# Attention, eight routed experts and a final feed-forward layer in one kernel: the first expert chosen two blocks earlier, the expert columns in ten parts

## The chip, the cores and the metric

One core of a Trainium2 chip runs the whole program in one launch. The metric is device time in microseconds; lower is better. The core has TensorE (PE, with its weight loads shown apart as PEld), VectorE (DVE), ScalarE (ACT), GpSimd (POOL) and SyncE (SP, which only issues transfers here). Each works through its own list of instructions in order.

## The reference, cut to what matters

```python
x   = attention(q, k, v)            # 4 x 576 tokens, 8 heads of 64; causal windows of 32 keys,
                                    # for half of the heads with a dilation of 4
logits = x @ w_gate                 # 2304 tokens, 8 experts
e_idx  = argmax(logits, axis=1)     # one expert for each token
out[mask_e] = gate_w * eom * (relu(x[mask_e] @ w1[e]) @ w2[e])     # 512 -> 1024 -> 512
return square(relu(out @ w_in)) @ w_out                            # 512 -> 2048 -> 512
```

Which tokens go to which expert is known only when the logits are; the lists of tokens are made on the chip. With the default seed of the reference, sorted after the expert that is chosen first, the experts get 427, 363, 309, 308, 271, 266, 188 and 172 tokens if the choice is made after 15 blocks of attention; after 13 blocks another expert leads, and the order is 363, 427, 309, 308, 271, 266, 188, 172.

## The kernel before, in words

**Attention** (lines 311 to 734) goes over 18 blocks of 128 tokens in a software pipeline. In one turn of the loop, for block i: `tr` transposes the probabilities on PE, `ex` takes the exponential of block i+1 on ACT, `qk` makes the scores of block i+2 (32 matmuls on PE, then the mask, the row maximum on DVE and the subtraction of the maximum on GpSimd), `xt` transposes the result of block i-1, and `pv` multiplies by the values (PE) and normalises (`pv_x`, DVE). `store` writes the result x to a table in HBM through SP's queue, `load_q`, `load_k`, `load_v` bring inputs through the same queue.

**Routing** is done for groups of blocks (`GROUPS`, line 29). When a group is complete, `lg` multiplies by the gate weights, `route1` to `route3` find each token's expert (DVE, one exponential on ACT), `route4` counts on PE, `route5` turns counts into places in the lists (some eleven small DVE instructions), `scatter` writes one record a token into the table `meta_d` with indirect DMAs from GpSimd (one for each of the group's two or four columns), and `route6` carries the counts on.

**The first expert early.** The last three blocks are written out by hand (lines 680 to 733). Once blocks 0 to 14 are routed, `choose` (line 180) names the expert with most tokens so far. Its weights are loaded (`load_w`: raw pieces of 512 KB through SP, three buffers; `conv_w`: high half on ACT, low half on DVE), and the first 256 tokens of its list are fetched: `meta_load(0)` reads the list, `gather(0)` fetches the rows of x by an indirect DMA for each 128, `scale(0)` multiplies them by the gate (DVE), `transposes(0)` transposes them on PE and splits them into high and low halves. Then the experts' matmuls begin.

**The experts** (from line 736) work on `WD`, a list of parts of columns (tokens): two of 256 for the first expert, then one part for each other expert, of a fixed width from `WIN` in order of size. A part is 96 matmuls for `up` (8 x 12) and 96 for `down` (4 x 24), each with its own 128 x 128 weights and as many columns as the part has: with every product in three matmuls of float32r halves (`mm3`). In a part's steps the next expert's weights are converted and units of the last layer's weights are prepared (`plan`). The second part's list is read (`meta_load(1)`) and gathered when the last group of blocks has been scattered; the last layer follows, 2304 tokens in blocks of 384.

```python
WIN = [512, 384, 336, 320, 304, 288, 256, 256]
WD = [(0, 0, HALF), (0, HALF, HALF)] + [(r, 0, WIN[r]) for r in range(1, E)]   # HALF = 256
```

An expert with more tokens than its window sends the rest to a slow loop after the end (`spilled`). With the counts above it has no turn, before or after the change.

Of the kernel before, what the change touches and what calls it, by code (L numbers as in the profile page):

```python
# [37 lines left out]

WIN = [512, 384, 336, 320, 304, 288, 256, 256]
HALF = WIN[0] // 2  # L40
MS = NT + 256
YC = sum(WIN) + 128
NEG = -8.0e9
# [9 lines left out]
def attention_experts_kernel(ctx: ExitStack, tc: tile.TileContext, qB, kB, vB, wg, wE, wF, consts, rows, ids, out):  # L53
# [29 lines left out]
    nspill = cpool.tile([1, 1], I32, name="nspill")  # L83
    mt = cpool.tile([P, E + 1, 3, 4], I32, name="mt")

# [18 lines left out]

    WD = [(0, 0, HALF), (0, HALF, HALF)] + [(r, 0, WIN[r]) for r in range(1, E)]
    NW = len(WD)
    reg = {}

# [86 lines left out]
    def order_steps(tp):  # L195
# [46 lines left out]
        yield v.reduce_sum(out=low, in_=f16, axis=AX.X)  # L242
        yield v.tensor_scalar(out=low, in0=low, scalar1=float(HALF), scalar2=None, op0=ALU.is_lt)
        big = row([1], "big1")
# [66 lines left out]
    def attention():  # L311
# [94 lines left out]
        def qk(i):  # L406
            qk_mm(i)
            qk_x(i)
# [28 lines left out]
        def qk_b(i):  # L437
            sm = sm_t[i]
            mx = wk.tile([P, H], F32, tag="mx", name="mx")
            nc.vector.reduce_max(out=mx, in_=sm, axis=AX.X)  # L440
            nc.gpsimd.tensor_tensor(out=sm, in0=sm, in1=mx.unsqueeze(2).to_broadcast([P, H, 64]), op=ALU.subtract)

# [83 lines left out]

        def t3(g, name, dt=F32):
            return wk.tile([P, 4, E], dt, tag=name, name=name)[:, 0:COLS[g]]

        def t2(g, name, dt=F32):  # L530
            return wk.tile([P, 4], dt, tag=name, name=name)[:, 0:COLS[g]]

# [6 lines left out]
        def route1(g):  # L539
            n, c = rows_of(g), COLS[g]  # L540
            ls, d = wk.tile([P, 4, 32], F32, tag="ls", name="ls")[:, 0:c], t3(g, "d")
# [25 lines left out]

        def route4(g):

            ls, e, oh = rt[g]  # L570
            c = COLS[g]
            rk = ps_1.tile([P, 5, E], F32, tag="rk", name="rk")
# [62 lines left out]
        ends = {g[-1] + 1: n for n, g in enumerate(GROUPS)}  # L635
        for i in range(EARLY):
            tr(i)
            ex(i + 1)
            qk(i + 2)
            t = (i + 2) % LAP  # L640
            n = i + 2 - t + LAP
            if t == 2 and n < NB:
                load_k(n, 2)
            if t == 4 and n + 2 < NB:
                wrap()
                load_k(n + 2, min(3, NB - n - 2))
            if i > 0 and i % 2 == 0:
                store(i - 2, 2)
            if i % 2 == 0 and i + 6 < NB:
                load_q(i + 6, 2)  # L650
            if i == 0:
                load_consts()
            if i == 3:
                clear()
            if i == 3:
                nc.vector.tensor_copy(tri, tri32)
                nc.vector.tensor_copy(cs[:, 0, :], io8)
            for a, g in ((2, ends.get(i - 2)), (4, ends.get(i - 3))):
                if g is not None and g < NG - 3:
                    scatter(g, range(a - 2, min(a, COLS[g])))  # L660
            if i > 0:
                xt(i - 1)
            g = ends.get(i - 1)
            if g is not None:
                route4(g)
            pv(i)
            if i % 2 == 1 and i + 3 < NB:
                load_v(i + 3, 2)
            if i in ends:
                lg(ends[i])  # L670
                route1(ends[i])
                route2(ends[i])
                route3(ends[i])
            if g is not None:
                route5(g)
                route6(g)
                if g == NG - 3:
                    scatter(g)

        i, g = EARLY, NG - 2  # L680
        store(i - 1, 1)
        tr(i)
        qk_mm(i + 2)
        xt(i - 1)
        qk_a(i + 2)
        ex(i + 1)
        lg(g)
        route1(g)
        pv_mm(i)
        route2(g)  # L690
        route3(g)
        qk_b(i + 2)
        tr(i + 1)
        cnt = route4(g)
        pv_mm(i + 1, True)
        route5(g)
        scatter(g)
        ex(i + 2)
        pv_x(i)
        choose(wk, cnt)  # L700
        reg["e", 0] = loaded(e0_t, SPE, E - 1, PERM)[0]
        reg["p", 0] = loaded(e0_t, POOLE, E - 1, PERM)[0]
        load_w(0, 0)
        meta_load(0, nc.sync, "e")
        load_w(0, 1)
        gather(0)
        tr(i + 2)
        xt(i)
        pv_x(i + 1)
        pv_mm(i + 2)  # L710
        xt(i + 1)
        route6(g)
        pv_x(i + 2)
        xt(i + 2)
        store(i, 1)
        lg(g + 1)
        warm(6)
        conv_w(0, 0)
        route1(g + 1)
        route2(g + 1)  # L720
        route3(g + 1)
        load_w(0, 2, "p")
        cnt = route4(g + 1)
        warm(2)
        load_w(0, 3)
        store(i + 1, 1)
        store(i + 2, 1)
        scale(0)
        transposes(0, lambda k: ps_1.tile([P, 1024 if k == 2 else 512], F32, tag=("pt", "lg", "o", "xt")[k], name="xT"))
        conv_w(0, 1)  # L730
        route5(g + 1)
        scatter(g + 1)
        nc.vector.tensor_copy(cs[:, 1, :], cnt[0:1, :])
        return st

    def experts():
        attention().close()
        st = ExitStack()
# [50 lines left out]
        def up(w, f):  # L789
# [11 lines left out]
            h_t[w, f] = (h, l)  # L801
            if f % 2 and w:
                free.append(w_t.pop((r, f // 2)))

        def down(w, c):
            r, _, n = WD[w]
            s = w_t[r, 4 + c]
# [6 lines left out]
            nc.scalar.copy(out=y[:, :n], in_=p[:, :n])  # L814
            at = slice(HALF * w, HALF * w + n) if w < 2 else ds(oa[r], n)
            nc.scalar.dma_start(out=yT_d[P * c:P * c + P, at], in_=y[:, :n])
            if w:
                free.append(w_t.pop((r, 4 + c)))

        def ids_out(w):  # L820
            r, s0, n = WD[w]
            at = slice(HALF * w, HALF * w + n) if w < 2 else ds(oa[r], n)
            nc.scalar.dma_start(out=idc_d[at, :], in_=meta_d[ds(reg["a", r] * MS + s0, n), :])
# [99 lines left out]
        CSTEPS = (1, 3, 5, 8, 8, 9, 10, 11)  # L923
        USTEPS = {1: (7,), 2: (4,), 3: (7,), 4: (4,), 5: (7,), 6: (4,), 7: (2, 7), 8: (3, 5, 8, 9)}
        units = [(m, p) for m in range(16) for p in range(2)]
        plan, taken = [], 0
        for w in range(NW):
            at = {i: [] for i in range(12)}
            if w == 0:
                for c, i in enumerate((1, 3, 5, 6, 7, 8)):  # L930
                    at[i].append(("w", 0, 2 + c))
# [8 lines left out]
        flat = [s for at in plan for i in range(12) for s in at[i]] + [("u",) + u for u in units[taken:]]  # L940
        state = dict(issued=2, done=0)

# [27 lines left out]

        meta_load(1)
        gather(1)
        issue()
        for w in range(NW):
            for f in range(8):
                up(w, f)
                step(w, f)
                if f == 3 and w > 1:
                    ids_out(w)
                if f == 5 and 0 < w < NW - 1:  # L980
                    scale(w + 1)
                if f == 0 and w + 1 == NW:
                    load_y(0)
            for c in range(4):
                down(w, c)
                if w == 0 and c == 1:
                    scale(1)
                if w == 0 and c == 2:
                    transposes(1, xbank4)
# [198 lines left out]
```

## Time and profile before

| | |
|---|---|
| time, median of 3 runs | 790.93 us (787.83 to 794.71) |
| profiled execution | 794.1 us, span 792.4 us |
| mean granted TensorE clock | 0.974 |
| PE busy | 736.1 us (93%), 5363 matmuls |
| PEld busy | 670.6 us (85%) |
| DVE, ACT, POOL busy | 437.1, 328.7, 94.6 us |
| transfers | 110.54 MB, 140 GB/s mean |

All times of rows are microseconds from the start of the span. A PE row's length is modelled and holds the time through the array, so back-to-back matmuls overlap in the rows; the distance between the starts of two rows is what one costs. "Idle before <-" names what ended an engine's wait. A window's row gives busy time and count for each engine, then the granted clock as a share of full speed.

### The profile page before, as it was taken

How to read it: one execution, taken by the hardware profiler on the slowest of the kernel's cores; microseconds unless marked ns; L12 is line 12 of the kernel's file. 1: busy time of each engine (PE TensorE's matmuls, PEld its weight loads, DVE VectorE, ACT ScalarE, POOL GpSimd, SP SyncE). 2: the span in 40 equal slices, each digit the busy share in tenths (PEclk: the TensorE clock that was granted, in tenths of full speed). 3: DMA queues.
4: the chain of work that ended last, by engine and by line, in shares of the span. 5: the costliest groups of instructions: out<-in, count | busy, mean ns of one | idle time of the engine just before them, and what ended most of it. 6: DMA issues, size and time to landing. Idle time of an engine off the chain costs nothing. (4 is left out here: it accounts for less than half of the span.)

```text
span 792.4 us, 13859 instructions
## 1 busy us (share of the span) xinstructions
PE 736.1 (93%) x5363; PEld 670.6 (85%) x5363; DVE 437.1 (55%) x888; ACT 328.7 (41%) x647; POOL 94.6 (12%) x104
## 2 busy tenths in 40 slices
PE   8767759899999999999999999999999999999993
PEld 5555539899999999999999989999889888889992
DVE  7656636477566566777677787762333333332421
ACT  3433324364454555655555555552222222222320
POOL 5234414320110110000000000000100000010101
PEclk9999869899999999999999999999999999999997
DMA  8999457474666667765444334330302012030201
GB/s 275 296 274 255 119 171 191 137 244 142 223 185 200 201 200 218 213 216 166 129 159 134 124 116 160 107 119 1 97 23 91 29 45 76 10 111 1 81 1 43
DMA packets 55073, 110.54 MB, mean 140 GB/s; under 512 B 9497, under 2 KB 30874, under 8 KB 55002
## 3 DMA queue, kind: packets, MB, share of 16 engines
q1 hardware_dynamic: 45338, 93.35, 39.0%
q0 software_dynamic: 4192, 10.77, 3.8%
q10 hardware_dynamic: 5472, 5.48, 2.0%
q8 instruction: 44, 0.72, 0.4%
q14 instruction: 27, 0.22, 0.1%
HBM read 89.62 MB, written 20.00 MB: 138 GB/s over the span
## 5 line engine op out<-in xcount | busy, mean ns | idle before, releaser
L785 PE MATMUL hp<-xh,slot 128*128 128x384 f32 (+5 forms) x672 | 216.4, 322 | 1.2 <-DVE hl L800 1.2
L787 PE MATMUL hp<-xh,slot 128*128 128x384 f32 (+5 forms) x672 | 216.1, 322 | 0.0
L786 PE MATMUL hp<-xl,slot 128*128 128x384 f32 (+5 forms) x672 | 215.7, 321 | 0.0
L785 PEld LDWEIGHTS hp<-xh,slot 128*128 128x128 f32 x672 | 127.7, 190 | 4.8 <-DVE hl L800 1.4
L786 PEld LDWEIGHTS hp<-xl,slot 128*128 128x128 f32 x672 | 127.7, 190 | 3.2 <-DVE xl L158 0.2
L787 PEld LDWEIGHTS hp<-xh,slot 128*128 128x128 f32 x672 | 127.6, 190 | 0.0
L872 DVE SCALAR_TENSOR_TENSOR g<-hp,r 128x384 f32<-128x384 f32 x96 | 53.2, 554 | 120.3 <-ACT r L871 119.8
L899 PE MATMUL op<-slot,gh 128*128 128x512 f32 x288 | 112.5, 390 | 1.9 <-ACT gh L874 1.9
L901 PE MATMUL op<-slot,gl 128*128 128x512 f32 x288 | 113.9, 395 | 0.0
L900 PE MATMUL op<-slot,gh 128*128 128x512 f32 x288 | 113.3, 393 | 0.0
L124 DVE TENSOR_TENSOR slot<-raw,slot 128x1024 fp32r<-128x1024 f32 x64 | 77.8, 1224 | 52.3 <-ACT slot L123 52.2
L871 ACT ACTIVATE r<-hp 128x384 f32<-128x384 f32 x96 | 46.9, 489 | 142.1 <-PE hp L787 141.7
L786 PE MATMUL yp<-hl,slot 128*128 128x256 f32 (+5 forms) x288 | 87.0, 302 | 1.3 <-DVE hl L800 1.2
L785 PE MATMUL yp<-hh,slot 128*128 128x256 f32 (+5 forms) x288 | 88.1, 306 | 0.1
L787 PE MATMUL yp<-hh,slot 128*128 128x256 f32 (+5 forms) x288 | 86.6, 301 | 0.0
L876 DVE TENSOR_TENSOR gl<-g,gh 128x384 fp32r<-128x384 f32 x96 | 53.5, 557 | 44.0 <-ACT gh L874 43.4
L874 ACT CAST gh<-g 128x384 fp32r<-128x384 f32 x96 | 49.2, 513 | 62.9 <-DVE g L872 62.5
L913 POOL DMA_INDIRECT out<-os,idc x18 | 17.6, 976 | 469.3 <-DVE os L912 467.8
L123 ACT CAST slot<-raw 128x1024 fp32r<-128x1024 f32 x64 | 66.4, 1051 | 14.0 <-DMA raw<-in_wE 9.4
L901 PEld LDWEIGHTS op<-slot,gl 128*128 128x128 f32 x288 | 54.0, 188 | 12.5 <-DVE gl L876 1.2
L899 PEld LDWEIGHTS op<-slot,gh 128*128 128x128 f32 x288 | 54.1, 188 | 12.3 <-ACT gh L874 3.2
L900 PEld LDWEIGHTS op<-slot,gh 128*128 128x128 f32 x288 | 54.0, 188 | 9.7
(152 smaller groups left out, 879.8 us busy)
## 6 DMA issues: line engine op xcount, KB each, us to landing
raw<-in_wE SPq DMA_DIRECT2D x63, 512.0 KB, 4.0
raw<-in_wF SPq DMA_DIRECT2D x32, 512.0 KB, 3.7
yr<-yT_d SPq DMA_DIRECT2D x48, 192.0 KB, 3.3
vb<-in_vB SPq DMA_DIRECT2D x16, 520.0 KB, 8.4
part_d<-os SPq DMA_DIRECT2D x18, 256.0 KB, 2.0
raw<-part_d SPq DMA_DIRECT2D x18, 256.0 KB, 4.3
q<-in_qB SPq DMA_DIRECT2D x8, 512.0 KB
x_d<-x SPq DMA_DIRECT2D x22, 128.0 KB
```

Source lines behind the costliest of these rows:

```text
L123: nc.scalar.copy(out=hi, in_=raw)
L124: nc.vector.tensor_tensor(out=lo, in0=raw, in1=hi.bitcast(F32), op=ALU.subtract)
L785: nc.tensor.matmul(out=out, lhsT=wh, rhs=mh, start=first, stop=False)
L786: nc.tensor.matmul(out=out, lhsT=wh, rhs=ml, start=False, stop=False)
L787: nc.tensor.matmul(out=out, lhsT=wl, rhs=mh, start=False, stop=last)
L871: nc.scalar.activation(out=r, in_=p[:, :TB], func=ACTF.Relu)
L872: nc.vector.scalar_tensor_tensor(out=q, in0=p[:, :TB], scalar=0.0, in1=r, op0=ALU.max, op1=ALU.mult)
L874: nc.scalar.copy(out=h, in_=q)
L876: nc.vector.tensor_tensor(out=l, in0=q, in1=h.bitcast(F32), op=ALU.subtract)
L899: nc.tensor.matmul(out=o_t[j], lhsT=h[:, a], rhs=w[:, 0], start=first, stop=False)
L900: nc.tensor.matmul(out=o_t[j], lhsT=h[:, a], rhs=w[:, 1], start=False, stop=False)
L901: nc.tensor.matmul(out=o_t[j], lhsT=l[:, a], rhs=w[:, 0], start=False, stop=last)
```

## The change

- The groups become blocks 0-2, 3-6, 7-10, 11-12, 13-15 and 16-17. The first expert is chosen after block 12 (`CHOICE = 4`, `EARLY = 13`), and its first part holds 13 x 128 / 8 = 208 columns, which the leading expert has at least.
- The hand-written ending goes; all 18 blocks run in the loop. At block 14 the loop does `route4`, `route5`, `scatter` of group 3, `choose`, and `meta_load(0)` through GpSimd's queue. The list is gathered at the end of block 14; weights are loaded from there and the pieces 0 and 1 converted at the ends of blocks 15 and 16.
- For blocks 15 to 17 the subtraction of the row maximum moves from GpSimd to DVE. Of group 2 all four scatters come at once, at block 12.
- After the loop: `xt`, `lg` and `route1` to `route3` of the last group, then `scale(0)`, `transposes(0)` (into the two banks of the scores) and pieces 2 and 3. The eight `warm` matmuls there are gone. The last group's `route4` comes after the first expert's first eight-th of `up`, `route5` and `scatter` (two DMAs in place of four) after the second (`last_group`), `meta_load(1)` and `gather(1)` after the third.
- The windows become 464, 432, 344, 328, 304, 288, 264, 248, in ten parts: 208, 256, 216, 216, 344, 328, 304, 288, 264, 248.

```diff
-GROUPS = [range(0, 3), range(3, 7), range(7, 11), range(11, 13), range(13, 15), range(15, 18)]
+GROUPS = [range(0, 3), range(3, 7), range(7, 11), range(11, 13), range(13, 16), range(16, 18)]
...
-EARLY = GROUPS[NG - 1][0]
+CHOICE = 4
+EARLY = GROUPS[CHOICE][0]
-WIN = [512, 384, 336, 320, 304, 288, 256, 256]
-HALF = WIN[0] // 2
+WIN = [464, 432, 344, 328, 304, 288, 264, 248]
+FIRST = EARLY * P // E
...
-    WD = [(0, 0, HALF), (0, HALF, HALF)] + [(r, 0, WIN[r]) for r in range(1, E)]
+    WD = [(0, 0, FIRST), (0, FIRST, WIN[0] - FIRST)] + [(1, i * WIN[1] // 2, WIN[1] // 2) for i in range(2)] + [(r, 0, WIN[r]) for r in range(2, E)]
...
-            nc.gpsimd.tensor_tensor(out=sm, in0=sm, in1=mx..., op=ALU.subtract)
+            (nc.vector if i > EARLY + 1 else nc.gpsimd).tensor_tensor(out=sm, in0=sm, in1=mx..., op=ALU.subtract)
...
-        for i in range(EARLY):
+        cnt = None
+        for i in range(NB):
             tr(i)
-            ex(i + 1)
-            qk(i + 2)
+            if i == EARLY + 1:
+                cnt = route4(CHOICE - 1)
+            if i + 1 < NB:
+                ex(i + 1)
+            if i == EARLY + 1:
+                route5(CHOICE - 1)
+                scatter(CHOICE - 1)
+                choose(wk, cnt)
+                reg["p", 0] = loaded(e0_t, POOLE, E - 1, PERM)[0]
+                meta_load(0)
+            if i + 2 < NB:
+                qk(i + 2)
+            if i == EARLY + 1:
+                route6(CHOICE - 1)
...
+            if i == EARLY + 1:
+                reg["e", 0] = loaded(e0_t, SPE, E - 1, PERM)[0]
+                load_w(0, 0)
+                load_w(0, 1)
+                load_w(0, 2)
+                gather(0)
+            elif i == EARLY + 2:
+                conv_w(0, 0)
+                load_w(0, 3)
+            elif i == EARLY + 3:
+                conv_w(0, 1)
+                load_w(0, 4)
+        g = NG - 1
+        store(NB - 1, 1)
+        xt(NB - 1)
         lg(g)
         route1(g)
...
+        scale(0)
+        banks = [ps_s.tile([P, 512], F32, tag="s", name="xT") for _ in range(2)]
+        transposes(0, lambda k: banks[k // 2][:, 256 * (k % 2):256 * (k % 2) + 256])
+        conv_w(0, 2)
+        load_w(0, 5)
+        conv_w(0, 3)
+        load_w(0, 6)
...
-        meta_load(1)
-        gather(1)
         issue()
         for w in range(NW):
             for f in range(8):
                 up(w, f)
+                if w == 0 and f < 2:
+                    last_group(f, ps.tile([P, 5, E], F32, tag="o", name="rk", bufs=5) if f == 0 else None)
                 step(w, f)
+                if w == 0 and f == 2:
+                    meta_load(1)
+                    gather(1)
```

## Rows read from the trace of the kernel before

**Rows 1.** Windows by stage: length, then busy (count) of each engine, clock, DMA share, GB/s.
```profile
98.01:115.00 16.99, 7.73 (x55) 4.37 (x54) 4.67 (x17) 2.99 (x8) 2.67 (x3) 0.70 0.75 200
115.00:138.18 23.18, 23.01 (x169) 22.43 (x168) 15.90 (x44) 11.42 (x21) 8.38 (x9) 0.89 0.62 159
138.18:143.93 5.75, 1.74 (x9) 1.55 (x9) 1.93 (x6) 1.16 (x4) 4.55 (x7) 0.71 0.60 179
148.41:172.74 24.33, 24.33 (x206) 24.33 (x205) 17.28 (x37) 14.51 (x26) 3.99 (x3) 1.00 0.54 171
172.74:207.31 34.57, 34.57 (x206) 34.50 (x205) 22.64 (x42) 16.62 (x27) 3.52 (x3) 1.00 0.63 207
375.51:781.71 406.20, 402.03 (x2018) 362.92 (x2016) 198.91 (x363) 152.79 (x310) 16.66 (x18) 1.00 0.25 80
```

**Rows 2.** Timeline of PE, attention's last blocks: start, length, line, operation, [idle before <-releaser].
```profile
75.84 1.09 PE L469 MATMUL o<-vb,pts 128*32 128x130 f32 x32
...
81.20 0.38 PE L453 MATMUL pt<-ident,pr 128*128 128x128 f32 x2 [3.46 <-issue]
...
96.09 1.92 PE L469 MATMUL o<-vb,pts 128*32 128x130 f32 x32
...
99.80 0.66 PE L507 MATMUL xt<-ident,x 128*128 128x128 f32 x4 [0.74 <-ACT xT L510]
100.39 1.59 PE L522 MATMUL lg<-xT,wg_sb 128*32 128x128 f32 x24
...
115.00 0.58 PE L785 MATMUL hp<-xh,slot 128*128 128x256 f32 x1
```

**Rows 3.** Timeline of DVE, SP's queue and POOL: the chosen expert, its list, its rows.
```profile
96.40 0.14 DVE L193 CAST e_t<-e 1x1 int32<-1x1 f32 x1
97.28 0.38 SPq L116 DMA_DIRECT2D raw<-in_wE  x1
100.27 0.39 SPq L136 DMA_DIRECT2D mt<-meta_d  x1
105.13 1.05 POOL L142 DMA_INDIRECT xg<-x_d,mt  x1 [8.16 <-DMA x_d<-x]
113.53 0.48 DVE L152 TENSOR_SCALAR xg<-xg,mt 128x512 f32<-128x512 f32 x1 [2.98 <-DMA xg<-x_d,mt]
```

**Rows 4.** Timeline of POOL and DVE: last scatter, second list, second gather.
```profile
123.09 0.92 POOL L615 DMA_INDIRECT meta_d<-idsb,di  x1 [0.30 <-issue]
129.38 0.76 POOL L136 DMA_DIRECT2D mt<-meta_d  x1 [5.36 <-DMA meta_d<-idsb,di]
...
141.98 0.49 DVE L152 TENSOR_SCALAR xg<-xg,mt 128x512 f32<-128x512 f32 x1 [1.72 <-DMA xg<-x_d,mt]
```

**Rows 5.** Timeline of DVE: a full-size step, a weight's low half, routing's first and last step.
```profile
82.73 0.69 DVE L434 TENSOR_TENSOR sm<-s,masks 128x512 f32<-128x512 f32 x1 [2.95 <-PE s L420]
...
104.01 1.23 DVE L124 TENSOR_TENSOR slot<-raw,slot 128x1024 fp32r<-128x1024 f32 x1 [4.68 <-ACT slot L123]
105.16 0.30 DVE L542 STREAM_TRANSPOSE ls<-lg 96x128 f32<-96x128 f32 x1
...
106.50 0.20 DVE L565 TENSOR_TENSOR oh<-eq,m 96x32 bf16<-96x32 f32 x1
```

**Rows 6.** Weight loads by line (ns min/median/max); then starts of two neighbours, twice.
```profile
L453 PEld LDWEIGHTS pt<-ident,pr x72: 137/140/225, 11.9 to 93.3; 128*128 128x128 f32 x72
L785 PEld LDWEIGHTS hp<-xh,slot x672: 186/188/330, 115.0 to 772.5; 128*128 128x128 f32 x168
...
701.89 0.19 PEld L899 LDWEIGHTS op<-slot,gh 128*128 128x128 f32 x1 [1.03 <-ACT gh L874]
702.00 0.19 PEld L900 LDWEIGHTS op<-slot,gh 128*128 128x128 f32 x1
...
137.66 0.28 PE L785 MATMUL yp<-hh,slot 128*128 128x256 f32 x1
137.78 0.28 PE L786 MATMUL yp<-hl,slot 128*128 128x256 f32 x1
```

More of the change, by code (lines that the diff above doesn't have):

```diff
@@ L37 @@
 FF2 = 2048
-WIN = [512, 384, 336, 320, 304, 288, 256, 256]
-HALF = WIN[0] // 2
+WIN = [464, 432, 344, 328, 304, 288, 264, 248]
+FIRST = EARLY * P // E
 MS = NT + 256
-YC = sum(WIN) + 128
+YC = sum(WIN[:-1]) + WIN[1]
 NEG = -8.0e9
@@ L102, in attention_experts_kernel @@
     io32 = rowc[:, 4 * E + E * E:4 * E + E * E + NSPILL]
-    WD = [(0, 0, HALF), (0, HALF, HALF)] + [(r, 0, WIN[r]) for r in range(1, E)]
+    WD = [(0, 0, FIRST), (0, FIRST, WIN[0] - FIRST)] + [(1, i * WIN[1] // 2, WIN[1] // 2) for i in range(2)] + [(r, 0, WIN[r]) for r in range(2, E)]
     NW = len(WD)
+    ends_rank = [w + 1 == NW or WD[w + 1][0] != WD[w][0] for w in range(NW)]
     reg = {}
@@ L242, in order_steps @@
         yield v.reduce_sum(out=low, in_=f16, axis=AX.X)
-        yield v.tensor_scalar(out=low, in0=low, scalar1=float(HALF), scalar2=None, op0=ALU.is_lt)
+        yield v.tensor_scalar(out=low, in0=low, scalar1=float(FIRST), scalar2=None, op0=ALU.is_lt)
         big = row([1], "big1")
@@ L646, in attention @@
                 load_k(n + 2, min(3, NB - n - 2))
-            if i > 0 and i % 2 == 0:
+            if i > EARLY - 1:
+                store(i - 1, 1)
+            elif i > 0 and i % 2 == 0:
                 store(i - 2, 2)
@@ L658, in attention @@
             for a, g in ((2, ends.get(i - 2)), (4, ends.get(i - 3))):
-                if g is not None and g < NG - 3:
+                if g is not None and g < CHOICE - 2:
                     scatter(g, range(a - 2, min(a, COLS[g])))
@@ L673, in attention @@
                 route3(ends[i])
+            if i == EARLY:
+                pv_x(i)
             if g is not None:
                 route5(g)
+                if g >= CHOICE or g == CHOICE - 2:
+                    scatter(g)
                 route6(g)
[L677 to L686, printed above, removed]
+            if i == EARLY + 1:
[10 more added lines that the diff above has]
+                load_w(0, 4)
@@ L687, in attention @@
+        g = NG - 1
+        store(NB - 1, 1)
+        xt(NB - 1)
         lg(g)
         route1(g)
-        pv_mm(i)
         route2(g)
         route3(g)
[L692 to L727, printed above, removed]
-        scale(0)
@@ L736, in experts, with last @@
+        load_w(0, 6)
+        def last(what, rk=None):
+            if what == 0:
+                cs_t.append(route4(g, rk))
+            else:
+                route5(g)
+                scatter(g)
+                nc.vector.tensor_copy(cs[:, 1, :], cs_t[0][0:1, :])
+        cs_t = []
+        return st, last
     def experts():
-        attention().close()
+        st, last_group = attention()
+        st.close()
         st = ExitStack()
@@ L801, in up @@
             h_t[w, f] = (h, l)
-            if f % 2 and w:
+            if f % 2 and ends_rank[w]:
                 free.append(w_t.pop((r, f // 2)))
         def down(w, c):
-            r, _, n = WD[w]
+            r, s0, n = WD[w]
             s = w_t[r, 4 + c]
@@ L929, in experts @@
             if w == 0:
-                for c, i in enumerate((1, 3, 5, 6, 7, 8)):
-                    at[i].append(("w", 0, 2 + c))
+                for c, i in enumerate((4, 6, 7, 8)):
+                    at[i].append(("w", 0, 4 + c))
+            elif WD[w][0] == 1:
+                for c, i in enumerate(CSTEPS[1::2]):
+                    at[i].append(("w", 2, 4 * (w - 2) + c))
             elif w < NW - 1:
@@ L940, in experts @@
         flat = [s for at in plan for i in range(12) for s in at[i]] + [("u",) + u for u in units[taken:]]
-        state = dict(issued=2, done=0)
+        state = dict(issued=3, done=0)
         def issue():
@@ L985, in experts @@
                 down(w, c)
-                if w == 0 and c == 1:
+                if w == 0 and c == 2:
                     scale(1)
-                if w == 0 and c == 2:
                     transposes(1, xbank4)
```

36 lines of the change are left out of this document (20 added, 16 removed).

## The prediction

> **What bounds the kernel now.** I read the windows by stage first: from 148.41 to 781.71 us PE has hardly a pause, in the parts of the experts (windows of 24.33 and 34.57 us, [rows 1]) and in the last layer, which is 406.20 us long and which the change leaves alone. Whatever reaches this stretch sooner ends sooner, and whatever adds PE work to it ends later, one for one. Ahead of it are two holes. Between the end of attention's last value product (96.09 + 1.92 = 98.01) and the first expert matmul (115.00) lie 16.99 us with 7.73 us of PE work at a mean clock of 0.70 [rows 1, 2]. Between the third `down` of the first part (138.18) and the next one (143.93) lie 5.75 us with 1.74 us of work [rows 1]. Then the timelines say what each hole waits for. In the first it is a chain: the expert's number is known at 96.40, its list is asked for at 100.27, the first rows of x at 105.13, and DVE waits for the last of them until 113.53 [rows 3]. In the second it is the same chain for the second part: last scatter 123.09, list 129.38 (a wait of 5.36 us for the scatters' landing), last rows at 141.98 [rows 4].
>
> **Part 1: the first hole.** Up to block 13 both programs give PE the same list (its value product starts at 75.84), and the pause of 3.46 us in block 14's transposes, which waits for no engine ("issue"), should come again, so I start at its end, 81.20 + 0.38 = 81.58 [rows 2]; with `route4`'s small matmuls, some 0.4 us by my estimate, DVE gets work at 82.0. From there DVE is the fullest engine. Its queue up to the end of block 17's `pv_x`: small instructions, 11 of `route5`, 8 of `choose`, 2 of `route6`, 2 in each of four `pv_x`, 29 x 0.14 = 4.1 us (the length of `e_t`'s, [rows 3]); ten of full size (mask, maximum and the moved subtraction for blocks 16 and 17, four in `pv_x`) x 0.69 = 6.9 us; two low halves of weights x 1.23 = 2.5 us; `route1` to `route3` of group 4, 105.16 to 106.70, 1.5 us [rows 5]. Sum 15.0 us, so 97.0 if DVE never waits. It does wait: for block 15's `qk`, for the transposed x ahead of `lg`, for the last value product, and behind ACT, whose conversion of piece 0 waits for a load issued only after the choice, with block 16's copy of the probabilities queued behind it. I take 3 us for these waits together, between 0 and 6. End of attention's arithmetic: 100.0, two microseconds after the end of the last value product before.
>
> Then, as before, `xt` and `lg`: 99.80 to 101.98, 2.2 us [rows 2]; the routing steps 1.5 us [rows 5]; the first `scale` 0.48 us; and from the start of the second to the first matmul 113.53 to 115.00, 1.5 us [rows 2, 3]. New is that the transposes lie in the scores' two banks, and I expect the first `up` to take the first of these over: it then waits for two low halves of x, 0.6 us by my estimate from the 0.69 us of 512 columns. First expert matmul: 100.0 + 2.2 + 1.5 + 0.5 + 1.5 + 0.6 = 106.3, a gain of 8.7 us. Bounds: 103.3 to 109.3 with the waits.
>
> What covers the edits counted at nothing here: from the choice to the last `scale` it was 113.53 - 96.40 = 17.1 us [rows 3]. The choice is now at 82.0 + 19 x 0.14 = 84.7, so the rows lie there by about 101.8, and DVE comes to the second `scale` at 104.2: about 2 us of cover (more, if the rows come without the 8.16 us in which the first gather stood behind a store of x, [rows 3]: the stores of blocks 0 to 12 are out by then); if it is gone each further microsecond is paid. GpSimd's queue holds `meta_load(0)` and both gathers behind the landing of group 3's two scatters (and group 2's four, sent together at block 12). Behind that wait stand only group 4's four scatters, which nobody needs before the lists are read; the subtractions that would have stood there are on DVE, counted above. SP waits for the expert's number at block 14, and behind it stand three loads and the stores of blocks 14 to 17. All inputs were asked for by block 13, and the second gather, the first reader of those stores, comes over 15 us later. The load of piece 2 leaves GpSimd's queue for SP's; SP has nothing urgent then. The dropped `warm` matmuls lay in PE's pauses and cost nothing then; without them the first `up` starts at the low clock, which it also did before (0.89 in the stage from 115.00, [rows 1]). The last group's own tiles take away a wait for buffers in a place that DVE no longer has, and I count nothing for it.
>
> **Part 2: the second hole.** Before, the last scatter starts 123.09 - 115.00 = 8.1 us after the first expert matmul, and the second part starts 143.93 - 115.00 = 28.9 us after it [rows 2, 4]. Now `route5` stands behind two `up`s, and on DVE behind two low halves of weights (2.5 us) and the first steps' halves; with two scatters in place of four I again get 8.2 us. From the scatter to the list was 6.3 us with four in the queue; with two I take 5.3, between 4.3 and 6.3. The rest, 129.38 to 143.93, stays. So 28.0 us, a gain of 0.9 (0 to 2). The first part's matmuls lie under this chain: 168 of them took 23.18 us [rows 1]. That this part has 208 columns and not 256 is therefore worth nothing: it makes the hole longer, not the end earlier.
>
> **Part 3: the columns.** A part of 256 columns takes 24.33 us, one of 384 takes 34.57 [rows 1]: 0.080 us a column and 3.85 us for the part itself (transposes, and what each matmul costs beside its columns). From the second part on, the widths 384, 336, 320, 256, 256 (1552 in five parts) become 216, 216, 344, 328, 264, 248 (1616 in six); 256, 304 and 288 stay. With the same price for a column that is 64 x 0.080 + 3.85 = +9.0 us.
>
> But three of the new parts are narrower than 256, and no f32r matmul of the trace is. What they cost is bounded below by the line through 256 and 384 (+9.0 us). Above, the nearest row with fewer columns is the plain f32 transpose: four of 128 columns in 0.66 us [rows 2], 1.29 ns a column, which would make a matmul of 216 columns 279 ns instead of 120 and add some 100 us. I take neither end, because the weight loads tell more. Each matmul has its own weights. The f32r loads take 188 ns where plain f32 ones of the same size take 140, and where no matmul holds them back, two follow each other at 701.89 and 702.00 [rows 6]: one in 0.11 us, and the matmuls of 256 columns come at 137.66 and 137.78, one in 0.12. At 256 columns load and matmul are thus about equal; below, the load remains. So I price a part under 256 columns like one of 256: 256, 256, 344, 328, 264, 256 is 1704, and 152 x 0.080 + 3.85 = +16.0 us.
>
> The Trainium skill (TensorE: Matmul & The Clock Gate, section "LDWEIGHTS (loading the stationary operand)") gives a load as columns divided by 1.2, that is 107 ns for 128 columns, which speaks against the ten parts, since it doesn't fall with the part's width. The trace's 0.11 us agrees. Taken as the whole price of a matmul it would save 13 ns on 2 x 192 matmuls and 4 ns on 192 against my 120 ns, 5.7 us, and the sum of part 3 would be +10.3.
>
> **Sum.** -8.7 - 0.9 + 16.0 = +6.4 us. Against the profiled execution, 794.1 us (span 792.4, the rest around it unchanged), that is 800.5; this execution stands 3.2 us above the median of 790.93, so for the median I write 797.3. Spill turns cost nothing: with the reference's counts neither set of windows leaves any token over (427 fit into 432).
>
> **Rivals.** A, the forecast, 0.68: narrow parts cost as 256; own range 793 to 802 from the waits of part 1, the chain of part 2 and 1 us in part 3.
>
> B, 0.17: narrow parts cost their load alone, 0.11 us (0.01 us less on 2 x 192 matmuls, +12.2), or their columns alone (+9.0), instead of +16.0. Then gain and price nearly cancel: 790.3 to 793.5. For it: 0.11 against 0.12 us in [rows 6]. Against: the 0.01 us between them looks like a cost of every matmul, whatever bounds it.
>
> C, 0.04: narrow f32r matmuls go at the rate of the plain f32 rows; about 900 us or more. Against it: these rows belong to another data type.
>
> D, 0.11, clearly slower: the wait moves into the loop. Place: ACT's conversion of piece 0 and GpSimd's list read, both of which now stand inside blocks 14 to 16 and wait for transfers, while DVE has 15.0 us to do. Price: each microsecond by which the loads or the list come late is one on the first expert matmul. At 110.5 instead of 106.3 the sum is +10.6, 801.5 us; above 107.8 the loss passes 1%. For it: before, the first low half began 6.7 us after its load's issue (97.28 to 104.01, [rows 3, 5]), and now three loads are issued together. Against it: only the last blocks' values load beside them.
>
> That the early choice brings nothing at all (the first matmul at 115) would need the gather 10 us later than counted; it is within D's tail.
>
> **Range and chances.** 7.9 us (1%) is what a measurement can tell from none. A lies above that in about 3 of 10 cases: 0.20; with C and D 0.35, and I give slower 0.37. Faster by over 1% needs B together with the earliest first matmul (103.3) and the shortest chain: 0.04. Within 1%: 0.59. The range takes A with its bounds, B's lower side down to 789, and D up to 804.
>
> **What would show it.** The first f32r matmul at 106.3 (103 to 109), with DVE nearly without pause from 82 to 100; the second part 28 us later; the two windows of 216 columns at 24 to 25 us each and starts of matmuls 120 ns apart (21 to 23 us would be B); DVE's second `scale` waiting for no transfer. Wrong it would be if PE paused inside the ten parts (ACT or DVE late for narrow parts), or if the rows came later than `lg`.

## The result and the profile after

The changed kernel takes 800.41 us (median of 4 runs, 798.92 to 801.24) against 790.89 in the runs beside it: ratio 1.0116, 95% interval 1.0069 to 1.0163. Forecast were 797.3 us in a range of 789 to 804, with "within 1%" as the likeliest class; the sum was +6.4 us, the runs say +9.5.

The two profiled runs are only 4.8 us apart (798.92 us, span 797.2, against 794.10, span 792.4): that of after is the fastest of its four runs, that of before one of the slower. Windows by stage of after, in the columns of [rows 1]: first hole (from the end of the last value product), second hole, the second part, the two parts of 216 columns, the last layer (to the end of PE's last matmul; to that point it is 403.96 us before, since the window in [rows 1] ends 2.2 us behind it).

```profile
101.39:108.95 7.56, 2.50 (x46) 1.87 (x45) 5.22 (x26) 1.97 (x7) 3.96 (x4) 0.90 0.52 142
130.60:136.37 5.77, 1.74 (x9) 1.54 (x9) 1.46 (x4) 1.12 (x4) 5.38 (x8) 0.86 0.54 143
139.95:163.81 23.86, 23.86 (x203) 23.86 (x202) 16.07 (x35) 13.92 (x26) 3.14 (x3) 1.00 0.60 173
163.81:188.56 24.75, 22.80 (x202) 22.43 (x201) 15.93 (x37) 10.44 (x24) 2.21 (x2) 1.00 0.58 184
188.56:211.24 22.68, 22.68 (x206) 22.68 (x205) 10.95 (x23) 9.53 (x20) 3.45 (x3) 1.00 0.45 138
380.84:784.28 403.44, 401.70 (x2018) 363.08 (x2016) 198.75 (x363) 152.57 (x310) 15.98 (x17) 1.00 0.25 80
```

The first hole is 7.56 us long where it was 16.99, but it begins at 101.39 and not at 98.01: part of it has moved into attention. The second is as long as before (5.77 against 5.75), though its clock is higher. Timeline of PE, DVE, ACT, POOL and SP's queue in after, from the choice to the second part (answers to [rows 2 to 4]):

```profile
80.77 0.14 DVE L197 CAST e_t<-e 1x1 int32<-1x1 f32 x1
85.11 1.44 SPq L120 DMA_DIRECT2D raw<-in_wE  x3
90.56 0.78 POOL L140 DMA_DIRECT2D mt<-meta_d  x1 [8.20 <-DMA meta_d<-idsb,di]
92.94 1.04 ACT L127 CAST slot<-raw 128x1024 fp32r<-128x1024 f32 x1 [7.18 <-DMA raw<-in_wE]
93.90 0.58 ACT L459 COPY pts<-pt 128x512 f32<-128x512 f32 x1
94.53 1.96 PE L473 MATMUL o<-vb,pts 128*32 128x130 f32 x32 [6.36 <-ACT pts L459]
95.68 1.07 POOL L146 DMA_INDIRECT xg<-x_d,mt  x1 [4.34 <-DMA x_d<-x]
104.76 0.25 DVE L550 STREAM_TRANSPOSE lsl<-lg 128x64 f32<-128x64 f32 x1 [0.70 <-PE lg L526]
105.96 0.92 DVE L156 TENSOR_SCALAR xg<-xg,mt 128x512 f32<-128x512 f32 x2
108.95 0.54 PE L799 MATMUL hp<-xh,slot 128*128 128x208 f32 x1 [1.46 <-DVE xl L162]
117.95 1.02 POOL L624 DMA_INDIRECT meta_d<-idsb,dil  x1 [0.31 <-issue]
121.14 0.77 POOL L140 DMA_DIRECT2D mt<-meta_d  x1 [2.16 <-DMA meta_d<-idsb,dil]
134.42 0.49 DVE L156 TENSOR_SCALAR xg<-xg,mt 128x512 f32<-128x512 f32 x1 [3.04 <-DMA xg<-x_d,mt]
139.95 0.29 PE L799 MATMUL hp<-xh,slot 128*128 128x256 f32 x1
```

The choice is known 15.6 us earlier than in [rows 3] and the rows of x are waited for no longer: both scalings go together at 105.96. In their place PE waits, in this trace, 6.36 us in block 16, for the copy of the probabilities that stands on ACT behind the conversion of piece 0, which waits 7.18 us for its load. The first expert matmul starts at 108.95 (115.00 before, 106.3 forecast).

**A yardstick for the runs.** PE has hardly a pause behind the start of the second part, so a run's time less that start should be a constant of the kernel. It nearly is. Before, it is 794.10 - 148.41 = 645.69 in the first trace, and 645.53 and 645.19 in two later ones with the same parts (e9, e11): mean 645.47. With the ten parts it is 798.92 - 139.95 = 658.97, then 657.84, 658.72 and 658.64 (e8, e10, e3): mean 658.54 (e2, e5 and e6, below, give 658.3 to 659.6). So the ten parts cost **13.1 us** (forecast +16.0). What is left of the medians is the front: the second part starts at 790.89 - 645.47 = 145.4 before and at 800.41 - 658.54 = 141.9 after, a gain of **3.6 us** (forecast 9.6). The pair of traces (148.41 and 139.95) shows 8.5 us for it, because these two runs are drawn from opposite ends of their kernels' times.

### The profile page after: what moved, and what is told of

The parts are those of the page before. It is cut to its first block, busy times and chain, and to the rows that moved or that the text cites. A ratio compares the mean times of both kernels' runs of the same rounds, so it can differ in the third digit from the quotient of the medians.

```text
span 797.2 us, 14309 instructions
## 1 busy us (share of the span) xinstructions
PE 738.1 (93%) x5555; PEld 676.7 (85%) x5555; DVE 441.0 (55%) x902; ACT 330.5 (41%) x663; POOL 95.1 (12%) x104
## 5 line engine op out<-in xcount | busy, mean ns | idle before, releaser
L799 PE MATMUL hp<-xh,slot 128*128 128x384 f32 (+9 forms) x704 | 223.4, 317 | 3.9 <-DVE hl L814 2.4
L801 PE MATMUL hp<-xh,slot 128*128 128x384 f32 (+9 forms) x704 | 222.9, 317 | 0.0
L800 PE MATMUL hp<-xl,slot 128*128 128x384 f32 (+9 forms) x704 | 222.5, 316 | 0.0
L799 PEld LDWEIGHTS hp<-xh,slot 128*128 128x128 f32 x704 | 133.9, 190 | 7.7 <-DVE hl L814 3.0
L800 PEld LDWEIGHTS hp<-xl,slot 128*128 128x128 f32 x704 | 133.9, 190 | 3.0
L801 PEld LDWEIGHTS hp<-xh,slot 128*128 128x128 f32 x704 | 133.8, 190 | 0.0
L914 PE MATMUL op<-slot,gh 128*128 128x512 f32 x288 | 113.4, 394 | 0.0
L800 PE MATMUL yp<-hl,slot 128*128 128x216 f32 (+8 forms) x320 | 93.4, 292 | 2.6 <-DVE hl L814 2.6
L799 PE MATMUL yp<-hh,slot 128*128 128x216 f32 (+8 forms) x320 | 94.4, 295 | 0.1
L801 PE MATMUL yp<-hh,slot 128*128 128x216 f32 (+8 forms) x320 | 92.9, 290 | 0.0
L127 ACT CAST slot<-raw 128x1024 fp32r<-128x1024 f32 x64 | 66.5, 1050 | 16.8 <-DMA raw<-in_wE 12.2
L913 PEld LDWEIGHTS op<-slot,gh 128*128 128x128 f32 x288 | 54.2, 188 | 11.8 <-ACT gh L888 2.7
L800 PEld LDWEIGHTS yp<-hl,slot 128*128 128x128 f32 x320 | 61.1, 191 | 3.6 <-DVE hl L814 3.6
```

What stands on the lines that cost most here:

```text
L127: nc.scalar.copy(out=hi, in_=raw)
L799: nc.tensor.matmul(out=out, lhsT=wh, rhs=mh, start=first, stop=False)
L800: nc.tensor.matmul(out=out, lhsT=wh, rhs=ml, start=False, stop=False)
L801: nc.tensor.matmul(out=out, lhsT=wl, rhs=mh, start=False, stop=last)
L913: nc.tensor.matmul(out=o_t[j], lhsT=h[:, a], rhs=w[:, 0], start=first, stop=False)
L914: nc.tensor.matmul(out=o_t[j], lhsT=h[:, a], rhs=w[:, 1], start=False, stop=False)
```

## The experiments

Ratios are to the kernel before on the same chip, with their 95% intervals; "second part" and "first matmul" are starts in the trace.

**e3_cols_only and e8_after_again: the account.** e3 is the kernel before with the ten parts alone, e8 the changed kernel once more.

```diff
 e3, against before
-WIN = [512, 384, 336, 320, 304, 288, 256, 256]
+WIN = [512, 432, 344, 328, 304, 288, 264, 248]
-WD = [(0, 0, HALF), (0, HALF, HALF)] + [(r, 0, WIN[r]) for r in range(1, E)]
+WD = [(0, 0, HALF), (0, HALF, HALF)] + [(1, i * WIN[1] // 2, WIN[1] // 2) for i in range(2)] + [(r, 0, WIN[r]) for r in range(2, E)]
```

> The kernel before, with the choice after 15 blocks and its hand-written ending as they were, and only the columns changed: parts of 256, 256, 216, 216, 344, 328, 304, 288, 264, 248. Theory 1 (the ten parts' price is their own, apart from the early choice): from the second part to the last layer 240.9 us instead of 227.1, 13.8 us more, about 804.7 us. Rival (the price comes with the early choice, by weights or lists that arrive later): clearly less, 791 to 798 us.

> The changed kernel unaltered, for a second trace. Theory 1 (its front ends when the rows land, and that moves with the pauses in which PE waits for no engine and with transfers): first expert matmul later than in the first trace, 109 to 114, from the second part on the same 240.9 us within 0.5; ratio to the kernel before 1.010 to 1.016. Rival (the first trace is typical, and the median is above it for another reason): first matmul at 108 to 110.

e3: 806.07 us, 1.0162 (1.0125 to 1.0198), or 12.8 us; from the second part to the last layer 239.91 us against 227.10. e8: 802.61 us, 1.0119 (1.0086 to 1.0152). Columns alone are thus as dear as the yardstick says, and everything else in the change takes back 0.0043 of the ratio, 3.4 us (the two intervals together leave some 4 us either way, so this pair alone doesn't show a gain). By the yardstick the second part starts at 793.95 - 645.47 = 148.5 and 802.61 - 658.54 = 144.1 on e8's chip, a gain of 4.4 us. Timeline of PE and DVE in e8:

```profile
76.03 0.34 PE L526 MATMUL lg<-xT,wg_sb 128*32 128x64 f32 x5 [0.36 <-issue]
79.25 0.44 PE L526 MATMUL lg<-xT,wg_sb 128*32 128x64 f32 x4 [1.13 <-issue]
80.68 0.27 PE L526 MATMUL lg<-xT,wg_sb 128*32 128x64 f32 x1 [0.99 <-issue]
85.81 0.14 DVE L197 CAST e_t<-e 1x1 int32<-1x1 f32 x1
102.72 0.69 DVE L489 TENSOR_TENSOR x<-o,rr 128x512 f32<-128x512 f32 x1
104.65 0.69 PE L526 MATMUL lg<-xT,wg_sb 128*32 128x64 f32 x28 [0.23 <-ACT xT L513]
107.83 0.25 DVE L550 STREAM_TRANSPOSE lsl<-lg 128x64 f32<-128x64 f32 x1 [2.94 <-remote]
112.55 0.54 PE L799 MATMUL hp<-xh,slot 128*128 128x208 f32 x1 [1.33 <-DVE xl L162]
```

Two pauses are new beside the first trace. The logits of block 13 come in pieces ("issue"), so that the choice is known 5 us later (in e10 too, at 85.33). And behind the last logits, whose row ends at 105.34, DVE starts only at 107.83. The profile names no engine there ("remote"), but the semaphore events of the trace tell what DVE waits for: the semaphore that PE's matmuls raise. It rises at 107.80, 2.46 us behind the end of the last logits' row, where the median lag in this trace is 0.014 us. So it is PE's signal that comes late. As the end of a PE row is modelled, the trace doesn't tell whether the matmuls or only their signal were late. The first matmul is at 112.55, not 108.95.

**e2_conv_late and e5_loads_behind: ACT's wait taken away.** e2 converts pieces 0 and 1 a block later; e5 also sends pieces 1 and 2 through GpSimd's queue behind the gather, and converts piece 1 only after the transposes.

```diff
 e2, against after
-            elif i == EARLY + 2:
+            elif i == EARLY + 3:
...
-            elif i == EARLY + 3:
+            elif i == EARLY + 4:
 e5, besides
-                load_w(0, 1)
-                load_w(0, 2)
+                load_w(0, 1, "p")
+                load_w(0, 2, "p")
```

> The changed kernel, but pieces 0 and 1 of the first expert's weights are converted one block later (at the ends of blocks 16 and 17). Theory 1 (the 6.36 us in which PE waits for block 16's copied probabilities are ACT's wait for the raw piece ahead of that copy): the pause goes, the first expert matmul is next bound by the landing of its rows, asked for at 95.68 and 97.05, so about 105 instead of 108.95, and the time falls by 4 us, to about 796.4. Rival (the front is bound by DVE's work or by the list, and the pause only hides that): first matmul within 1.5 us of 108.95, time the same.

> The changed kernel, with the raw pieces 1 and 2 of the first expert's weights asked for through GpSimd's queue behind the gather instead of through SP's at the choice, and pieces 0 and 1 converted later (after block 16, and after the transposes). Theory 1 (from choice to rows it now takes 23 to 25 us and not the 17.1 of before, because three raw loads of 512 KB run beside the list and the rows): choice to second scale falls to 17 to 20 us, the first expert matmul comes at 104 to 107, about 4 us are gained, 796 us. Rival (the wait for the list and the rows is that of small indirect transfers themselves): still 23 us or more, no gain, 800 us.

e2: 801.63 us, 1.0117 (1.0080 to 1.0154); e5: 801.98 us, 1.0106 (1.0075 to 1.0138). No gain is seen, though the intervals leave some 4 us either way. The 6.36 us are gone in e2, and attention's arithmetic ends at 101.4 (102.6 in the first trace), but its timeline of DVE and PE shows what ends last instead:

```profile
103.23 1.07 PE L526 MATMUL lg<-xT,wg_sb 128*32 128x64 f32 x28 [0.51 <-ACT slot L127]
108.13 0.25 DVE L550 STREAM_TRANSPOSE lsl<-lg 128x64 f32<-128x64 f32 x1 [3.96 <-remote]
109.34 0.87 DVE L156 TENSOR_SCALAR xg<-xg,mt 128x512 f32<-128x512 f32 x2
109.87 1.65 PE L171 MATMUL xT<-ident,xg 128*128 128x128 f32 x8 [5.57 <-DVE xg L156]
112.86 0.54 PE L799 MATMUL hp<-xh,slot 128*128 128x208 f32 x1 [1.34 <-DVE xl L162]
```

Nobody waits for the rows: both scalings run as soon as DVE gets there. In e5 the gather follows the request for the list after 2.5 us (93.80 to 96.30) where it took 5.1 in after and 4.6 in e8, so the loads did lie in the way; whether of the list or of a store of x isn't shown, since the gather's last wait in after and e8 is for such a store. DVE's pause is 4.50 us, the first matmul at 111.85.

**e1_one432 and e4_both: the second expert in one part.** One part of 432 columns in place of two of 216; e4 is e1 with e2's edit.

```diff
-WD = [..., (1, i * WIN[1] // 2, WIN[1] // 2) for i in range(2), (r, 0, WIN[r]) for r in range(2, E)]
+WD = [..., (r, 0, WIN[r]) for r in range(1, E)]      # tiles of xh, xl, hh, hl 432 wide
```

> The changed kernel, but with the second expert's 432 columns in one part instead of two of 216 (the split halves of the inputs and hidden values get tiles of 432 columns; to make room, tri32 shares a raw buffer and three work tiles have one buffer fewer). Theory 1 (a part costs its weight loads: 192 matmuls at no less than about 0.11 us, whatever its columns, and a fixed share): the two parts of 216 took 24.76 and 22.68 us; one of 432 is priced by the line through 256 and 384 at 24.33 + 176 x 0.080 = 38.4 us, so 9.0 us less than the changed kernel, about 791.4 us. Theory 2 (columns alone are paid, and the changed kernel's loss lies at the front): only the fixed 3.85 us go, about 796.5 us.

> The edits of the first two together: one part of 432 and the conversions one block later. Theory 1: both gains add, 800.4 - 9.0 - 4.0 = 787.4 us, below the kernel before. Rival (the earlier start is eaten by a later wait): 791 us or more.

e1: 800.68 us, 1.0088 (1.0050 to 1.0127); e4: 797.99 us, 1.0062 (1.0036 to 1.0089). The part of 432 takes 38.90 us where the two took 24.75 + 22.68 = 47.43. Of these 8.5 us the part ahead gives 1.6 back (25.46 us instead of 23.86: it now transposes 432 columns and not 216). The yardstick falls by less, from 658.5 to 655.5 and 654.8, because the last layer got longer: from its first matmul to the end of the run it is 421.4 and 420.2 us in e1 and e4 (420.6 in e7 and e12, below) and 417.6 to 419.1 in the ten traces without a part of 432. PE doesn't wait longer there; its 512-column matmuls start on average 232 ns apart in place of 230, its 384-column ones 175.8 in place of 175.1. These kernels also have wider tiles and fewer work buffers; which of it does this was not tested. Neither theory's time came. By ratio e1 can't be told from the changed kernel, whose interval overlaps with its own; e4 lies about half a per cent lower, with intervals that still overlap at their ends, and its rival (791 us or more) held.

**e6_last_group and e11_before_last: the second hole alone.** The last group's places (`route5`) and scatter go ahead of the scaling of the first expert's rows: in e11 in the kernel before, and nothing else; in e6 in the changed kernel, where `route4` goes with them and the second list and gather are asked for ahead of the first expert matmul, as they are in the kernel before.

```diff
 e11, against before
-        scale(0)
-        transposes(0, ...)
-        conv_w(0, 1)
         route5(g + 1)
         scatter(g + 1)
         nc.vector.tensor_copy(cs[:, 1, :], cnt[0:1, :])
+        scale(0)
+        transposes(0, ...)
+        conv_w(0, 1)
```

> The changed kernel, with the last group's counting, places and scatters done right after its routing, ahead of scale and transposes of the first part, and the second list and gather asked for before the first expert matmul. Theory 1 (the second part starts when the chain scatter, list, rows is through, and the first part's 208 columns only lie under it): the chain begins some 9 us sooner, the 5.8 us hole before the second part goes, 5 to 7 us are gained less up to 2 us of DVE ahead of scale, about 795 us. Rival (the second part is bound by its own conversions or by the first part's matmuls): less than 2 us.

> The kernel before, with the last group's choice and scatter issued ahead of the scaling of the first expert's rows, and nothing else: no early choice, nine parts as before. Theory (the second hole is the chain scatter, list, rows of the second part and nothing else; with the scatter early it is gone, as with the change): the second part starts 24 to 26 us after the first expert matmul instead of 33.4, the first expert matmul 1.5 to 3 us later, ratio 0.991 to 0.995. Rival (VectorE's work ahead of the scaling costs as much as the hole, since without the early choice it all lies on the chain): first expert matmul 6 us or more later, ratio 0.998 to 1.003.

e6: 799.66 us, 1.0065 (1.0035 to 1.0095). e11: 786.60 us, **0.9909** (0.9881 to 0.9938), the fastest kernel of this study and faster than both. Timeline of POOL, DVE and PE in e11:

```profile
109.23 0.49 DVE L152 TENSOR_SCALAR xg<-xg,mt 128x512 f32<-128x512 f32 x1 [2.34 <-DMA xg<-x_d,mt]
111.45 0.92 POOL L615 DMA_INDIRECT meta_d<-idsb,di  x1 [0.30 <-issue]
112.18 0.49 DVE L152 TENSOR_SCALAR xg<-xg,mt 128x512 f32<-128x512 f32 x1 [2.47 <-DMA xg<-x_d,mt]
116.33 0.76 POOL L136 DMA_DIRECT2D mt<-meta_d  x1 [3.96 <-DMA meta_d<-idsb,di]
133.68 0.88 DVE L152 TENSOR_SCALAR xg<-xg,mt 128x512 f32<-128x512 f32 x2 [0.29 <-issue]
138.79 0.28 PE L785 MATMUL hp<-xh,slot 128*128 128x256 f32 x1
```

DVE's steps for the last group cost nothing here: it waits for the first rows all the same, 2.34 us where it was 3.35. The last scatter starts at 111.45 where it was 123.09 [rows 4], nothing waits for the second rows any more, and the second part comes 138.79 - 113.66 = 25.1 us behind the first matmul instead of 33.4. In e6 it comes 24.8 us behind it. e6 is some 3 to 4 us below e8 on the same chip (the intervals overlap at their ends), where 5 to 7 were expected. Its first matmul is at 115.39 (112.55 in e8); 1.2 us of that are the last group's steps, which here do lie on the chain: from the last logits' transpose to the scaling it is 2.40 us instead of 1.20.

**e9_before_again and e10_shift: whose pauses are they?** e9 is the kernel before once more, e10 the changed kernel with 40 one-element instructions ahead of everything on DVE that follows block 5.

```diff
+            if i == 5:
+                for _ in range(40):
+                    nc.vector.memset(idle, 0.0)
```

> The kernel before, unaltered, for a second trace. Theory (the pauses of PE and DVE in which they wait for no engine of the core belong to the stage, not to the early choice): such pauses of 0.4 to 4 us are there too between the last group's logits and the first expert matmul, and that matmul starts between 112 and 117 (first trace 115.00); columns behind it as before, last layer 227 us after the second part. Rival (the pauses come with the early choice alone): none over 1 us, first expert matmul within 1 us of 115.0.

> The kernel after, with 40 one-element memsets on VectorE at block 5, where VectorE has room: nothing else changes but the place of all later instructions in VectorE's list. Theory (the pause of 2.9 to 4.7 us at the transpose behind the last logits is the supply of instructions, at fixed places of the list): the pause is found at another instruction or is gone, and the first expert matmul starts 0 to 4 us earlier than the 112.55 of the second trace of after, or the loss shows elsewhere. Rival (the pause belongs to that transpose or to what it reads): again 2.9 to 4.7 us at the same instruction, time as after (ratio 1.012).

e9: one run of 795.65 us (before beside it: 794.50); first matmul 116.77, second part 150.12. e10: 800.26 us, 1.0083 (1.0051 to 1.0115). Timelines, e9 first:

```profile
80.20 0.38 PE L453 MATMUL pt<-ident,pr 128*128 128x128 f32 x2 [2.86 <-issue]
91.11 0.69 DVE L434 TENSOR_TENSOR sm<-s,masks 128x512 f32<-128x512 f32 x1 [3.63 <-remote]
91.09 0.37 ACT L509 COPY xT<-xt 128x256 f32<-128x256 f32 x1 [4.08 <-remote]
```

```profile
105.65 1.60 PE L527 MATMUL lg<-xT,wg_sb 128*32 128x64 f32 x32
110.23 0.25 DVE L551 STREAM_TRANSPOSE lsl<-lg 128x64 f32<-128x64 f32 x1 [4.28 <-remote]
114.95 0.54 PE L803 MATMUL hp<-xh,slot 128*128 128x208 f32 x1 [1.34 <-DVE xl L163]
```

The pauses are not the change's own: e9 has the one of PE at the same place as [rows 2], 2.86 us, and a second of 3.6 to 4.1 us on DVE and ACT at once, in attention's last blocks. (None lies between its last logits and the first expert matmul, where the theory looked for it.) They are not bound to a place in DVE's list either: the rival held, with the same instruction and 4.28 us. Traces of e1, e2 and e4 to e8, e10 and e12 have 2.9 to 4.7 us at this transpose; only the first trace of after has none there. What the pauses of DVE and ACT have in common is PE. Between 60 and 120 us the twelve traces of the experiments have 27 such "remote" pauses of over 1 us on DVE and ACT, and every one ends within 0.03 us of a rise of PE's semaphore, 1.5 to 4.5 us behind the end of PE's last row. The first traces of before and after have none.

**e7_all and e12_all_shift: the remedies together.** e7 joins e1, e5 and e6, with the windows of the kernel before for the last six experts and its banks for the first part's transposes; e12 adds e10's 40 instructions.

```diff
-WIN = [464, 432, 344, 328, 304, 288, 264, 248]
+WIN = [464, 432, 336, 320, 304, 288, 256, 256]
```

> The two edits before together with one part of 432 columns, the old windows 336, 320, 304, 288, 256, 256 for the others, and the transposes of the first part in banks that the first expert matmul does not take over. By theory 1: 800.4 - 4 - 5 - 6.8 (the part of 432 as its trace showed it) - 1.9 (24 columns by the line of 0.080 us) - 1.3 (the bank) = 781 us, below the kernel before by over 1%. Rival (the gains overlap: a faster front only waits for its rows): 788 to 793 us.

> The kernel of e7_all with the same 40 memsets at block 5. Theory (supply of instructions at fixed places): the pause of 4.5 us behind the last logits goes or moves off the chain, up to 4 us below e7_all (ratio 0.990 to 0.994). Rival (the pause belongs to the instruction): as e7_all, 0.9956.

e7: 791.21 us, 0.9956 (0.9934 to 0.9979); e12: 790.15 us, 0.9965 (0.9940 to 0.9989). With nine parts the early choice at last gains on the kernel before, but less than e11, which has no early choice: its second part starts at 139.66 and 135.30 (e11: 138.79), and behind it stand 653.4 us against 645.2. The medians, less these constants, put that start at 137.8 and 136.8, and at 141.4 in e11: the early choice does bring some 4 us at the front, and the wider part and the longer last layer that come with it cost 8. The 781 us that were expected of e7 did not come; its rival (788 to 793) held, as did e12's.

## Why the prediction came out where it did

The total lay in the range and the sign of the sum was right, but that is luck in part: two terms were too large, in opposite directions (the front by 6.0 us, the columns by 2.9). What was left over took the ratio to 1.0116, with an interval that straddles the bound of 1% between "no change" and "slower".

**Part 1 failed.** The first expert matmul comes at 113.4 to 116.8 in three traces with the front of before (before, e9, e3) and at 109.0, 112.6 and 115.0 in after, e8 and e10: 2.9 us between the means, 8.7 forecast. Two steps failed. The end of attention's arithmetic was put at 100.0; it is 102.6, 103.4 and 104.5. And from there to the first matmul it was to be 6.3 us; it is 6.4, 9.1 and 10.5.

The first step is "I take 3 us for these waits together, between 0 and 6". In the first trace of after, DVE is busy 11.01 of the 20.60 us from 82.00 to the end of attention's arithmetic (102.60), so it waits 9.6 (some of the 15.0 us of work counted lies ahead of 82.00, as the choice came at 80.77 and not at 84.7). Most of that is rival D's place, ACT behind the load of piece 0 (the three loads are issued at 85.11, the conversion starts at 92.94). D named the right wait at about its price (first matmul at 108.95; D had 110.5), but as a cause it doesn't hold the time: e2 removed it and gained nothing that can be seen. And 6.36 us is a draw: the same wait of PE is 2.34 us in e8 and 1.50 in e10, where the choice comes 5 us later but the loads only 1.1 to 1.6.

The second step lacks a term, in D as in the forecast: PE's late signal behind the last logits, a pause of 2.94 us in e8 and 4.28 in e10. I carried the 3.46 us of [rows 2] over unchanged and gave none to the stretch from block 15 on, where a second trace of before (e9) shows one of about 4 us. The cover counted for the rows did hold: no trace of the changed kernel waits for them. Nor do the banks explain it: from the second scaling (about 106.4) to the first matmul it is 2.5 us, 2.1 counted, and 3.1 in e8 and e10, where the granted clock is 0.50 in this stretch and not 0.69.

**Part 2 was right in its mechanism and too small.** The chain sets the hole, not the part's width, as e6 and e11 show: with the scatter early it vanishes, under 208 as under 256 columns. From the last scatter to the list it is 121.14 - 117.95 = 3.2 us with two scatters in the queue, 5.3 counted (3.1 in e8, 4.5 in e10; with four 6.3, and 5.1 and 5.5 in e9 and e3). From the first matmul to the `down` behind the hole, the forecast's own measure: 28.9 before (29.1 and 28.6 in e9 and e3); 27.4, 25.1 and 26.9 in after, e8 and e10, 28.0 forecast: 1.2 to 4.0 us gained, 0.9 counted. To the second part it is 33.4 before (32.3 in e3) and 31.0, 29.3 and 31.3. So 0.9 to 4.1 us are gained there. The medians give 3.6 us for the whole front, 4.4 on e8's chip and 7.3 on e10's, 9.6 forecast; little of part 1's 8.7 is left.

**Part 3 was 3 us too high: the narrow parts came cheaper than priced, and the removed ones had been dearer.** Starts of f32r matmuls in after, timeline of PE:

```profile
189.79 0.28 PE L801 MATMUL hp<-xh,slot 128*128 128x216 f32 x1
189.90 0.28 PE L799 MATMUL hp<-xh,slot 128*128 128x216 f32 x1
190.01 0.28 PE L800 MATMUL hp<-xl,slot 128*128 128x216 f32 x1
190.13 0.27 PE L801 MATMUL hp<-xh,slot 128*128 128x216 f32 x1
```

They are 0.11 us apart, the spacing of two loads in [rows 6], not the 0.12 of 256 columns: rival B's variant. The rule of the Trainium skill (TensorE: Matmul & The Clock Gate, "LDWEIGHTS (loading the stationary operand)"), 107 ns for such a load, agrees as a floor. But a part is more than its matmuls: the first of 216 columns takes 24.75 us, the other 22.68. The first has 1.95 us without PE work, and PE's timeline says what it waits for, the low halves of the hidden values that DVE makes:

```profile
169.28 0.38 PE L799 MATMUL hp<-xh,slot 128*128 128x216 f32 x1 [1.30 <-DVE hl L814]
179.02 0.37 PE L800 MATMUL yp<-hl,slot 128*128 128x216 f32 x1 [0.66 <-DVE hl L814]
```

That is the sign the prediction gave for being wrong, PE pausing inside the ten parts for DVE: 5.0 us of such waits from the second part to the last layer, 2.2 before. The six new parts took 159.2 us together and my prices made 159.4, but only because two errors cancel: the three narrow ones were 2.1 us cheaper, the other three (344, 328 and 264) 1.9 us dearer than the line. The line is too low for the removed parts as well. I priced those five by the line through 256 and 384, 143.4 us, and the trace of before had them; windows of before, its parts of 336, 320 and the last two:

```profile
207.31:239.14 31.83, 31.83 (x206) 30.86 (x205) 19.46 (x32) 16.21 (x27) 3.16 (x3) 1.00 0.60 190
239.14:269.98 30.84, 30.75 (x207) 29.59 (x206) 18.82 (x28) 15.86 (x27) 3.14 (x3) 1.00 0.65 196
325.75:351.24 25.49, 24.33 (x202) 23.99 (x201) 19.10 (x32) 15.51 (x30) 0.00 (x0) 1.00 0.73 213
351.24:375.51 24.27, 23.77 (x195) 23.26 (x194) 17.20 (x32) 13.91 (x29) 0.00 (x0) 1.00 0.56 185
```

With 34.57 for 384 [rows 1] that is 147.0, 3.6 more than the line. So 16.0 - 2.1 + 1.9 - 3.6 = 159.2 - 147.0 = +12.2 for these parts. That this is a figure of rival B is chance: B took 3.8 us off the narrow parts, which gave 2.1, and priced the rest as I did. The parts that kept their width changed too (288: 29.11 instead of 27.04; the second part 23.86 instead of 24.33), which makes the +13.8 of this pair of traces.

Rival C is out: no narrow matmul of 279 ns, where these start 0.11 us apart.

## What to carry to other kernels

Where a trace ends in a long stretch without pauses, a run's time less the start of that stretch is nearly a constant (within 0.5 us before, 1.1 us after): use it to split medians into front and stretch, since a single trace of the front is a draw (the first matmul of the same kernel starts at 108.95 in one and at 112.55 in another). Where the profile names no engine for a wait, look which semaphore ended it. Read the parts that a change removes from their own windows, and price only the new ones by a line. And look for the work that may simply stand earlier: a few lines moved under a wait that was there anyway (e11) gave 0.9%, where an early choice paid for with a tenth part lost 1.2%.

## What was not expected of the hardware

Pauses of 2.9 to 4.8 us in which DVE, and at times ACT with it, waits for a signal of PE that comes long after the row it belongs to. In e11 ACT stands still 4.75 us up to 88.08 and DVE 4.18 up to 88.09, for two different matmuls of PE whose rows end at 83.65 and 83.06; both signals come almost at once, at 88.06 and 88.00. Their cause is open. The ends of PE's rows are modelled, so PE may have stood still itself. A transfer of instructions lies inside the pause at the last logits in seven of its nine traces (in e8 at 105.2, e10 106.2, e12 104.6), but in e2 none does (the last is at 99.6), in e4 it ends as the pause begins, and after has one at 104.5 and hardly a pause. 40 instructions more on DVE's list moved nothing; a shift of PE's list, the next thing to try by these signals, was not tried. The Trainium skill (Runtime: NRT & Kernel Launch, "Instruction fetch mechanics") has the fetch of the next block of instructions mostly hidden; these traces neither show that it is nor that it isn't.
